# Attention and a 16-expert mixture in one kernel: combine weights computed from one set of instructions, two routing parts joined, key maxima kept from PSUM

## The chip, the cores and the metric

The kernel runs on one core of one Trainium2 chip. The metric is the device time of one launch in microseconds (us); lower is better. The core has five engines that run on their own and wait for one another through semaphores: PE (TensorE, matrix products; its weight loads are shown apart as PEld), DVE (VectorE), ACT (ScalarE), POOL (GpSimd) and SP (SyncE, which here issues nearly all transfers). Each engine takes its own instructions strictly in the order in which they were written for it, so an instruction that waits holds up everything behind it on that engine. Matrix products land in PSUM, a small memory of banks next to PE, and are read from there by ACT and DVE.

## The reference

Two stages. First an attention through 49 agents per batch (4 batches of 10048 tokens, 128 channels):

```
s  = scale * (agents @ k.T);  s -= max over keys;  a2k = exp(s) / (sum + 1e-9)
agent_v = a2k @ v
q2a = the same softmax of scale * (q @ agents.T), over the agents
x = q2a @ agent_v                       # 40192 x 128
```

Then a two-level mixture of experts on the 40192 rows of x: 4 groups with 4 experts each, hidden width 1024.

```
g_logits = x @ w_group;  g = argmax;  g_w = softmax(g_logits)[g]
e_logits = xg @ w_expert[g];  e = argmax;  e_w = softmax(e_logits)[e]
out[row] = g_w * e_w * (relu(x @ w1[g, e]) @ w2[g, e])
```

Both softmaxes carry the 1e-9 in the denominator. The product g_w * e_w is the *combine weight* of a row.

## The kernel before

**Tiling.** A batch has 79 blocks of 128 tokens; four blocks make a *tile* (512 tokens), so a batch has 20 tiles. A *unit* is one eighth of a tile's expert work: two 512-column products into a PSUM bank (`ph<-et,wbuf`), a ReLU on ACT (`hh<-ph`), its rounding rest on DVE (`hl<-ph,hh`), and, eight units later, twelve 128-column products (`po<-wbuf,hh` and `po<-wbuf,hl`). Inputs are handled as pairs of 16-bit numbers, a rounded part and a rest (`xh`, `xl`).

**Stages.** The first batch's keys and values are worked through alone (`front`). Then come the 20 tiles of the first, the second and the third batch (`SEQ = (1, 2, 3, 0)`), each with the one expert that most of that batch's tokens chose (`choose` finds it, loads its weights `w1f`, `w2f` and writes them into `wbuf` through `expert_split`). The fourth batch is sorted by expert, and its tiles run last, with the weights fetched per tile. All other work (keys and values of the later batches, queries, routing) is written between the units of the tiles by hand-made *lanes*: a list of generators with start and end times (`QUEUE`), advanced once per unit by `advance`, the lane furthest behind first. `k1` is the key lane of the second batch of `SEQ`, `q1` its query lane, `a1` its routing lane (`followed`). A scheduler of the framework then places each instruction on its engine, so the final order has to be read from the built program.

**Routing in parts.** `PARTS` and `SORTS` cut a batch's 20 tiles into parts: 0-2, 2-5, 5-10, 10-15, 15-20, or 0-5, 5-10, 10-15, 15-20 for the sorted batch. For each part `logits` computes the 20 router logits, `routing` the arg-max masks (`oh`), the first part's `choose` the batch's main expert, and `weigh` the combine weights `cw`. With n the token blocks of a part (8, 12 or 20), every DVE instruction of a part is 128 partitions by a small multiple of n. In `weigh` before, `numerators` runs once for the groups and once for the experts: subtract the largest, multiply by a per-token factor (both into a tile `rd`), exponentials on ACT (`rd<-rd,scb`); `fold` adds or takes the maximum of four rows in two steps (`rhg`, `rrg`, `rhe`, `rre`, `rhm`, `rrm`).

**Key scores.** Per chunk of ten blocks `key_scores` fills a PSUM bank (`at`) with 128x490 scores and ACT copies it to `S`. `key_largest`, one pipeline stage later, reduces the chunk over its ten blocks from `S` into `mch`; `key_max` reduces the eight chunk maxima (`mx<-mch`). PSUM tiles named `at` share three banks.

**Staging.** Key, query and expert loads share four staging buffers (tag `xf`: `xf<-kT`, `xf<-qT`, `w1f`); value loads and `w2f` share two (tag `vf`). SP issues all of them in one queue. `values_load(ei)` in `expert_load` makes SP read the chosen expert's number (`cei`) before it can issue `w1f`.

Of the kernel before, what the change touches and what calls it, by code (L numbers as in the profile page):

```python
# [10 lines left out]
F32 = mybir.dt.float32  # L11
F16 = mybir.dt.float16
I32 = mybir.dt.int32
AF = mybir.ActivationFunctionType
ALU = mybir.AluOpType
AX = mybir.AxisListType
# [4 lines left out]
P = 128  # L21
# [3 lines left out]
NA = 49  # L25
NG = 4
# [6 lines left out]
CT = 10  # L33
# [28 lines left out]
NOWN = B - 1  # L62
SORTED = SEQ[NOWN]
OT = -(-NT // TQ)
PARTS = ((0, 2), (2, 5), (5, 10), (10, 15), (15, OT))
SORTS = ((0, 5), (5, 10), (10, 15), (15, OT))
ST = 5 * TQ
ORDER = "kkkkkmkvkvqkqmvvqvvvv"
RATE = np.array([900.0, 1100.0])
# [66 lines left out]
def build(ctx, tc, qT, kT, v, agT, wr, w1, w2, cpk, out):  # L136
# [141 lines left out]
    def skewed(n, *stages):  # L278

        for i in range(n + len(stages) - 1):  # L280
            yield "chunk"
            live = [[stages[k](i - k), 0] for k in reversed(range(len(stages))) if 0 <= i - k < n]
            while live:
                moved = False
                for x in list(live):
                    if x[1] > clock[0] and not forced[0]:
                        continue
                    y = next(x[0], "end")
                    if y == 0:
                        continue  # L290
                    moved = True
                    if y == "end":
                        live.remove(x)
                        continue
                    if isinstance(y, int):
                        x[1] = clock[0] + y
                    yield
                if not moved:
                    yield 0
# [10 lines left out]
    def key_load(b, ci, early=None):  # L310

        st = state[b]
        if ci == 0:
            st["S"] = rt.tile([P, NT, NA], F32, name="S", tag="S")
            st["mch"] = sm.tile([P, len(chunks), NA], F32, name="mch")
            st["part"] = []
        st["k", ci] = yield from split_load("k", b, ci, early)
        yield

    def load_only(kind, b, ci):  # L320

        if (kind, b, ci) not in loaded:
            load_ahead((kind, b, ci))
        yield

    def key_scores(b, ci):

        st = state[b]
        S, mch = st["S"], st["mch"]
        t0, t1 = chunks[ci]  # L330
        xh, xl = st.pop(("k", ci))
        ps = bank()
        full = t1 - t0 - (1 if t1 == NT else 0)
        for t in range(t0, t1):
            scores(b, ps, xh, xl, t - t0, min(P, N - t * P))
            if t % 5 == 4:
                yield
        yield 1
        act.activation(S[:, t0:t0 + full], ps[:, 0:full * NA].rearrange("p (t a) -> p t a", a=NA), AF.Copy)
        if t1 == NT:  # L340
            act.activation(S[0:LAST, NT - 1], ps[0:LAST, full * NA:(full + 1) * NA], AF.Copy)
        yield

    def key_largest(b, ci):
# [9 lines left out]
    def key_max(b, c0, c1, early):  # L354

        st = state[b]
        i = len(st["part"])
        mx = sm.tile([P, NA], F32, name="mx")
        vec.tensor_reduce(out=mx, in_=st["mch"][:, c0:c1].rearrange("p c a -> p a c"), axis=AX.X, op=ALU.max)
        yield HOP  # L360
        ps = bank()
        pe.transpose(ps[0:NA, 0:P], mx, identf)
        yield HOP
        if i == 0:
            st["ma"] = sm.tile([NA, 3], F32, name="ma")
        ma = st["ma"][:, i:i + 1]
        vec.tensor_reduce(out=ma, in_=ps[0:NA, 0:P], axis=AX.X, op=ALU.max)
        dg = sm.tile([NA, NA], F32, name="dg")
        vec.tensor_scalar(out=dg, in0=identf[0:NA, 0:NA], scalar1=ma, scalar2=None, op0=ALU.mult)
        yield HOP  # L370
        ps = bank()
        pe.matmul(ps[:, 0:NA], ones[0:NA, :], dg, start=True, stop=True)
        yield HOP
        mb = sm.tile([P, 1, NA], F32, name="mb")
        vec.tensor_copy(out=mb[:, 0], in_=ps[:, 0:NA])
        if i == 0 and early:
            st["acc"] = bank(False)
        st["part"].append((c0, c1, mb, st["acc"][0:NA, i * (C + 1):(i + 1) * (C + 1)] if early else None))
        yield
# [107 lines left out]
    def agents(b):  # L487

        st = state[b]
        n = len(chunks)  # L490
        yield from skewed(n, lambda ci: load_only("k", b, ci), lambda ci: key_load(b, ci), lambda ci: key_scores(b, ci), lambda ci: key_largest(b, ci))
        yield from key_max(b, 0, n, False)
        yield from skewed(n, lambda ci: both(value_load(b, ci), value_less(b, ci)), lambda ci: value_exp(b, ci), lambda ci: value_split(b, ci), lambda ci: value_products(b, ci))
        yield
        acc = st["acc"]
        za = sm.tile([P, NA], F32, name="za2")
        vec.tensor_reduce(out=za, in_=acc[:, NA:(ZT + 1) * NA].rearrange("p (t a) -> p a t", a=NA), axis=AX.X, op=ALU.add)
        vec.tensor_scalar(out=za, in0=za, scalar1=1e-9 * ES, scalar2=None, op0=ALU.add)
        vec.reciprocal(out=za, in_=za)
        avT = sm.tile([P, NA], F32, name="avT")  # L500
        vec.scalar_tensor_tensor(out=avT, in0=acc[:, 0:NA], scalar=1.0 / VS, in1=za, op0=ALU.mult, op1=ALU.mult)
        yield
        yield from agents_scaled(b, avT)
# [116 lines left out]

    def followed(b):

        parts = SORTS if b == SORTED else PARTS
        first_part = 1 if b == SEQ[0] else 0
        moved = lambda f: lambda k: f(b, *parts[k + first_part])
        yield from skewed(len(parts) - first_part, *[moved(f) for f in ((part_logits, part_positions, part_rows) if b == SORTED else (part_logits, part_weights))])
        if b == SORTED:
            yield from order(b)
# [194 lines left out]
    def weigh(b, t0, t1):  # L823

        st = state[b]
        r = t0 // ST
        n, t = t1 - t0, slice(t0 - r * ST, t1 - r * ST)
        lg, ohf, g = st["lg", r], st["ohf", r], st["g", r]
        og = ohf[:, 0:NG, t]
        gm, zz, zr = [a[:, t] for a in g]  # L830

        def fold(src, op, name):
            h = sm.tile([P, 2, ST], F32, name="rh" + name)[:, :, 0:n]
            vec.tensor_tensor(out=h, in0=src[:, 0:2], in1=src[:, 2:4], op=op)
            r = sm.tile([P, ST], F32, name="rr" + name)[:, 0:n]
            vec.tensor_tensor(out=r, in0=h[:, 0], in1=h[:, 1], op=op)
            return r

        def numerators(x, largest):
            bc = lambda a: a.unsqueeze(1).broadcast_to([P, 4, n])  # L840
            d = sm.tile([P, 4, ST], F32, name="rd")[:, :, 0:n]
            vec.tensor_sub(out=d, in0=x, in1=bc(largest))
            vec.tensor_mul(out=d, in0=d, in1=bc(zr))
            yield HOP
            act.activation(d, d, AF.Exp, scale=st["scb"][:, 1:2])
            yield HOP
            return d

        x = sm.tile([P, NG, 4, ST], F32, name="rx")[:, :, :, 0:n]
        vec.tensor_mul(out=x, in0=lg[:, NG:NG + NE, t].rearrange("p (g e) t -> p g e t", g=NG), in1=og.unsqueeze(2).broadcast_to([P, NG, 4, n]))  # L850
        yield
        el = sm.tile([P, 4, ST], F32, name="rel")[:, :, 0:n]
        vec.tensor_add(out=x[:, 0:2], in0=x[:, 0:2], in1=x[:, 2:4])
        vec.tensor_add(out=el, in0=x[:, 0], in1=x[:, 1])
        yield
        sg = yield from numerators(lg[:, 0:NG, t], gm)
        sg = fold(sg, ALU.add, "g")
        yield
        se = yield from numerators(el, fold(el, ALU.max, "m"))
        se = fold(se, ALU.add, "e")  # L860
        yield
        vec.scalar_tensor_tensor(out=se, in0=se, scalar=1e-9, in1=zz, op0=ALU.add, op1=ALU.mult)
        vec.scalar_tensor_tensor(out=sg, in0=sg, scalar=1e-9, in1=se, op0=ALU.add, op1=ALU.mult)
        yield
        vec.reciprocal(out=sg, in_=sg)
        if t0 == 0:
            st["cw"] = sm.tile([P, NTP], F32, name="cw", bufs=3)
        cw, x0 = st["cw"][:, t0:t1], st["rows", r][:, t]
        vec.tensor_scalar(out=cw, in0=sg, scalar1=st["scb"][:, 1:2], scalar2=1.0 / W2S, op0=ALU.mult, op1=ALU.mult)
        vec.tensor_copy(out=x0[:, :, 2 * NA:2 * NA + 2].bitcast(F32), in_=cw.unsqueeze(2))  # L870
        sync.dma_start(out=erow[b].rearrange("(p t) c -> p t c", t=NTP)[:, t0:t1], in_=x0.bitcast(I32))
        yield
# [585 lines left out]
```

## Time and profile before

| | |
|---|---|
| time, median of 3 runs | 1004.84 us (1002.79 to 1009.59) |
| the profiled execution's own time | 1003.51 us |
| its span, first to last instruction | 1001.8 us |
| mean granted TensorE clock | 0.974 |
| PE, DVE, ACT, POOL busy | 90%, 78%, 64%, 43% of the span |

The 1.7 us between the profiled execution's time and its span lie outside the instructions. A granted clock below 1 means that the chip ran TensorE slower than it can for part of the time. "PE busy" is a modelled share: products are pipelined, so a busy PE need not be at its peak. The profile's line L131 is the helper through which all PE, DVE and ACT instructions pass, so rows are told apart by their tiles (`out<-in`), not by lines.

### The profile page before, as it was taken

How to read it: one execution, taken by the hardware profiler on the slowest of the kernel's cores; microseconds unless marked ns; L12 is line 12 of the kernel's file. 1: busy time of each engine (PE TensorE's matmuls, PEld its weight loads, DVE VectorE, ACT ScalarE, POOL GpSimd, SP SyncE). 2: the span in 40 equal slices, each digit the busy share in tenths (PEclk: the TensorE clock that was granted, in tenths of full speed). 3: DMA queues.
4: the chain of work that ended last, by engine and by line, in shares of the span. 5: the costliest groups of instructions: out<-in, count | busy, mean ns of one | idle time of the engine just before them, and what ended most of it. 6: DMA issues, size and time to landing. Idle time of an engine off the chain costs nothing.

```text
span 1001.8 us, 31196 instructions
## 1 busy us (share of the span) xinstructions
PE 900.1 (90%) x12947; PEld 718.8 (72%) x12948; DVE 784.7 (78%) x1758; ACT 636.3 (64%) x1086; POOL 426.2 (43%) x569
## 2 busy tenths in 40 slices
PE   3858898999878998989989989999999999999994
PEld 2735677787756776767777777787777877777884
DVE  5636899889949887799988889989987666666663
ACT  4507678776757765768776777666556565555552
POOL 3108644442641334553334443554555214444444
PEclk9977999999989999999999999999999999999998
DMA  9637514633454445362524420223535545554551
GB/s 308 188 105 209 170 62 122 188 92 100 122 172 124 140 123 148 89 185 64 149 89 128 142 70 26 104 72 100 174 120 200 184 148 183 188 178 149 174 194 33
DMA packets 107511, 138.14 MB, mean 138 GB/s; under 512 B 7479, under 2 KB 88186, under 8 KB 104160
## 3 DMA queue, kind: packets, MB, share of 16 engines
q1 hardware_dynamic: 102208, 125.75, 39.8%
q0 software_dynamic: 5152, 10.30, 3.1%
q8 instruction: 103, 1.69, 0.7%
q14 instruction: 48, 0.39, 0.1%
HBM read 96.83 MB, written 39.45 MB: 136 GB/s over the span
## 4 chain that ended last, share of the span: by engine, by line
PE 51%; DVE 27%; DMA 6%; POOL 5%; ACT 5%; issue 5%; SPq 1%; POOLq 0%; DVEq 0%; ACTq 0%
PE po L131 25%; PE ph L131 17%; DVE hl L131 10%; PE at L131 8%; POOL xl L267 4%; DVE vl L131 2%; DMA xf<-kT 2%; ACT hh L131 2%; DVE oh L131 1%; DVE oo L131 1%; DMA erow<-rows 1%; DVE rd L131 1%; DVE mq L131 1%; DVE ef L131 1%; DVE rx L131 1%
## 5 line engine op out<-in xcount | busy, mean ns | idle before, releaser
L131 DVE SCALAR_TENSOR_TENSOR hl<-ph,hh 128x512 f16<-128x512 f32 (+1 forms) x644 | 432.9, 680 | 122.7 <-ACT hh L131 121.2
L131 PEld LDWEIGHTS <-hh 128*128 128x128 f16 x5104 | 419.5, 98 | 146.9 <-issue 3.9
L131 PE MATMUL po<-wbuf,hh 128*128 128x128 f16 x5104 | 501.7, 220 | 0.0
L131 ACT ACTIVATE hh<-ph 128x512 f16<-128x512 f32 (+1 forms) x644 | 376.8, 592 | 194.5 <-PE ph L131 191.4
L131 PE MATMUL po<-wbuf,hl 128*128 128x128 f16 x2552 | 463.6, 220 | 0.0
L131 PE MATMUL ph<-et,wbuf 98*128 98x512 f16 (+2 forms) x1312 | 386.3, 377 | 26.9 <-DVE hl L131 25.1
L267 POOL TENSOR_TENSOR xl<-xf,xh 128x256 f16<-128x256 f32 x280 | 183.8, 691 | 211.1 <-ACT xh L131 168.1
L131 PEld LDWEIGHTS <-hl 128*128 128x128 f16 x2552 | 249.9, 98 | 0.8 <-issue 0.3
L131 PEld LDWEIGHTS <-wbuf 98*128 98x128 f16 (+1 forms) x1412 | 108.8, 100 | 53.0 <-issue 36.6
L1198 POOL DMA_INDIRECT out<-oo,er x82 | 80.2, 978 | 130.2 <-ACT hh L131 92.7
L975 POOL DMA_INDIRECT sorted_rows<-rows,slot x79 | 78.1, 989 | 63.1 <-ACT hh L131 44.4
L131 ACT ACTIVATE xh<-xf 128x1280 f16<-128x1280 f32 (+2 forms) x59 | 73.6, 1253 | 20.5 <-PE at L131 10.6
L693 POOL TENSOR_TENSOR rows<-ef,rows 128x245 f16<-128x245 f32 (+1 forms) x62 | 40.7, 678 | 70.5 <-ACT rows L131 69.2
L462 POOL TENSOR_TENSOR sl<-S,sh 128x245 f16<-128x245 f32 (+2 forms) x51 | 35.2, 714 | 79.7 <-ACT sh L131 70.0
L131 PE MATMUL at<-agh,xl 128*128 128x49 f16 x553 | 57.1, 187 | 8.9 <-POOL xl L267 8.8
L131 PEld LDWEIGHTS <-xh 128*128 128x128 f16 (+1 forms) x1164 | 55.8, 99 | 7.8 <-ACT xh L131 4.6
L131 PE MATMUL at<-agh,xh 128*128 128x49 f16 x553 | 57.1, 187 | 4.0 <-ACT xh L131 3.8
L131 PEld LDWEIGHTS <-xl 128*128 128x128 f16 (+1 forms) x582 | 48.9, 98 | 12.3 <-POOL xl L267 12.0
L131 PE MATMUL at<-agl,xh 128*128 128x49 f16 x553 | 56.7, 187 | 0.0
L131 ACT ACTIVATE et<-at 98x512 f16<-98x512 f16 (+2 forms) x81 | 47.0, 584 | 13.8 <-PE at L131 9.7
L131 DVE SCALAR_TENSOR_TENSOR vl<-vf,vh 128x640 f16<-128x640 f32 (+2 forms) x51 | 43.0, 849 | 5.5 <-ACT vh L131 5.5
L131 DVE TENSOR_TENSOR oo<-po,cw 128x512 f32<-128x512 f32 (+1 forms) x60 | 40.3, 672 | 3.4 <-PE po L131 3.4
(254 smaller groups left out, 940.9 us busy)
## 6 DMA issues: line engine op xcount, KB each, us to landing
wbuf<-wdr SPq DMA_DIRECT2D x22, 1024.0 KB, 4.7
vf<-v SPq DMA_DIRECT2D x28, 640.0 KB, 4.5
xf<-qT SPq DMA_DIRECT2D x28, 640.0 KB, 4.1
xf<-kT SPq DMA_DIRECT2D x23, 640.0 KB, 4.3
out<-oo SPq DMA_DIRECT2D x57, 256.0 KB, 3.3
erow<-rows SPq DMA_DIRECT2D x13, 510.0 KB
er<-sorted_rows SPq DMA_DIRECT2D x19, 256.0 KB, 3.1
wbuf<-kT SPq DMA_DIRECT2D x5, 640.0 KB, 5.3
```

The source lines that it names most:

```text
L131: return f(*a, **k)
L267: pool.tensor_sub(out=xl[:, a:z], in0=xf[:, a:z], in1=xh[:, a:z])
L462: pool.tensor_sub(out=sl[0:m, y][:, z], in0=x[:, z], in1=sh[0:m, y][:, z])
L693: pool.tensor_sub(out=x0[:, a:z, NA:2 * NA], in0=ef[:, a:z], in1=x0[:, a:z, 0:NA])
L975: ins = pool.indirect_dma_start(out=sorted_rows[:, :], out_offset=bass.IndirectOffsetOnAxis(ap=at, axis=0), in_=x, in_offset=None, bounds_ ...
L1198: ins = pool.indirect_dma_start(out=out, out_offset=bass.IndirectOffsetOnAxis(ap=to, axis=0), in_=y, in_offset=None, bounds_check=B * N - ...
```

## The change

Three edits:

1. `weigh` stacks the group logits and the expert logits of a part in one tile `rd` of eight rows. The factor is multiplied in once over eight rows, ACT takes one exponential over eight rows, and the two sums are folded together. The maximum of the expert logits is still taken by itself.
2. The parts 0-2 and 2-5 are kept apart only for the first batch. The second and the third batch now use 0-5, as the sorted batch did.
3. For the three later batches a running maximum `most` of 128x490 is kept: DVE copies the first chunk's scores out of PSUM and takes the elementwise maximum of it and of each later chunk's bank. `key_largest` is left out of their pipeline, which is a stage shorter, and `key_max` reduces `most` (128x490) once. The first batch keeps `mch`.

```diff
-PARTS = ((0, 2), (2, 5), (5, 10), (10, 15), (15, OT))
 SORTS = ((0, 5), (5, 10), (10, 15), (15, OT))
+PARTS = ((0, 2), (2, 5), *SORTS[1:])
...
     def key_scores(b, ci):
...
+        if "most" in st:
+            yield
+            for i, z, m in ((0, full, P), (full, t1 - t0, LAST)):
+                if z > i:
+                    o, x = st["most"][0:m, i:z], ps[0:m, i * NA:z * NA].rearrange("p (t a) -> p t a", a=NA)
+                    if ci == 0:
+                        vec.tensor_copy(out=o, in_=x)
+                    else:
+                        vec.tensor_tensor(out=o, in0=x, in1=o, op=ALU.max)
         yield
...
     def key_max(b, c0, c1, early):
...
-        vec.tensor_reduce(out=mx, in_=st["mch"][:, c0:c1].rearrange("p c a -> p a c"), axis=AX.X, op=ALU.max)
+        vec.tensor_reduce(out=mx, in_=(st["mch"][:, c0:c1] if early else st["most"]).rearrange("p c a -> p a c"), axis=AX.X, op=ALU.max)
...
     def agents(b):
-        yield from skewed(n, lambda ci: load_only("k", b, ci), lambda ci: key_load(b, ci), lambda ci: key_scores(b, ci), lambda ci: key_largest(b, ci))
+        yield from skewed(n, lambda ci: load_only("k", b, ci), lambda ci: key_load(b, ci), lambda ci: key_scores(b, ci))
...
     def followed(b):
-        parts = SORTS if b == SORTED else PARTS
+        parts = PARTS if b == SEQ[0] else SORTS
...
     def weigh(b, t0, t1):
...
+        four = lambda a: a.unsqueeze(1).broadcast_to([P, 4, n])
         x = sm.tile([P, NG, 4, ST], F32, name="rx")[:, :, :, 0:n]
         vec.tensor_mul(out=x, in0=lg[:, NG:NG + NE, t].rearrange("p (g e) t -> p g e t", g=NG), in1=og.unsqueeze(2).broadcast_to([P, NG, 4, n]))
         yield
-        el = sm.tile([P, 4, ST], F32, name="rel")[:, :, 0:n]
+        d = sm.tile([P, 2, 4, ST], F32, name="rd")[:, :, :, 0:n]
         vec.tensor_add(out=x[:, 0:2], in0=x[:, 0:2], in1=x[:, 2:4])
-        vec.tensor_add(out=el, in0=x[:, 0], in1=x[:, 1])
-        yield
-        sg = yield from numerators(lg[:, 0:NG, t], gm)
-        sg = fold(sg, ALU.add, "g")
-        yield
-        se = yield from numerators(el, fold(el, ALU.max, "m"))
-        se = fold(se, ALU.add, "e")
-        yield
+        vec.tensor_sub(out=d[:, 0], in0=lg[:, 0:NG, t], in1=four(gm))
+        yield
+        vec.tensor_add(out=d[:, 1], in0=x[:, 0], in1=x[:, 1])
+        h = sm.tile([P, 2, 2, ST], F32, name="rh")[:, :, :, 0:n]
+        vec.tensor_max(out=h[:, 0], in0=d[:, 1, 0:2], in1=d[:, 1, 2:4])
+        yield
+        vec.tensor_max(out=h[:, 1, 0], in0=h[:, 0, 0], in1=h[:, 0, 1])
+        vec.tensor_sub(out=d[:, 1], in0=d[:, 1], in1=four(h[:, 1, 0]))
+        yield
+        flat = d.rearrange("p k e t -> p (k e) t")
+        vec.tensor_mul(out=flat, in0=flat, in1=zr.unsqueeze(1).broadcast_to([P, 8, n]))
+        yield HOP
+        act.activation(flat, flat, AF.Exp, scale=st["scb"][:, 1:2])
+        yield HOP
+        vec.tensor_add(out=h, in0=d[:, :, 0:2], in1=d[:, :, 2:4])
+        sums = sm.tile([P, 2, ST], F32, name="rs")[:, :, 0:n]
+        vec.tensor_add(out=sums, in0=h[:, :, 0], in1=h[:, :, 1])
+        yield
+        sg, se = sums[:, 0], sums[:, 1]
         vec.scalar_tensor_tensor(out=se, in0=se, scalar=1e-9, in1=zz, op0=ALU.add, op1=ALU.mult)
```

**What it moves: SP's queue.** The rows below are SP's, in the key phase of the third batch (lane `k2`), where the second batch's expert is loaded before the change. `cei` is the chosen expert's number, `xf<-kT` a chunk of keys, `erow` the routing rows sent out, `oo` a finished tile.

```order
L237 DMA xf<-kT 128x1280 x2
L871 DMA erow_124<-rows 128x408
L1187 DMA out<-oo 128x4x128
L1079 TENSOR_LOAD cei
L1082 ISA
L1082 DMA w1f<-w 128x1024
L1083 ISA
L1083 DMA w2f<-w 128x8x128
L237 DMA xf<-kT 128x1280 x2
L416 DMA vf<-v 128x10x128
L237 DMA xf<-kT 128x1088
```

After the change the same load stands here, three finished tiles later (17 tiles are stored ahead of it instead of 14).

```order
L1194 DMA out<-oo 128x4x128
L428 DMA vf<-v 128x10x128
L1086 TENSOR_LOAD cei
L1089 ISA
L1089 DMA w1f<-w 128x1024
L1090 ISA
L1090 DMA w2f<-w 128x8x128
L237 DMA xf<-qT 128x1280
L237 DMA xf<-qT 128x1088
L1194 DMA out<-oo 128x4x128
L237 DMA xf<-kT 128x1280
L428 DMA vf<-v 128x10x128
```

Before, three key chunks stood behind the expert's load; after, the keys of that batch are all loaded ahead of it, and two query chunks and then values stand behind it.

**What it moves: the expert's weights on DVE.** The rows are DVE's around the writing of the second batch's weights (`wbuf_120`; `w1` halves first, then the halves of `w2`). Before:

```order
L131 TENSOR_TENSOR wbuf_120<-at,wbuf_120 128x512
L131 SCALAR_TENSOR_TENSOR wbuf_120<-w2f,wbuf_120 128x4x128
L131 TENSOR_TENSOR oo<-po,cw 128x512
L131 SCALAR_TENSOR_TENSOR hl<-ph,hh 128x512 x2
L131 SCALAR_TENSOR_TENSOR wbuf_120<-w2f,wbuf_120 128x4x128
L131 SCALAR_TENSOR_TENSOR hl<-ph,hh 128x512
```

After (128x384 is the size of the batch's last, shorter tile):

```order
L131 TENSOR_TENSOR wbuf_120<-at,wbuf_120 128x512
L131 TENSOR_REDUCE mq<-at 128x10
L131 SCALAR_TENSOR_TENSOR hl<-ph,hh 128x384
L131 TENSOR_TENSOR ef<-at,mq 128x490
L131 COPY rows<-cw 128x20
L131 SCALAR_TENSOR_TENSOR vl<-vf,vh 128x640
L131 SCALAR_TENSOR_TENSOR hl<-ph,hh 128x384 x2
L131 SCALAR_TENSOR_TENSOR wbuf_120<-w2f,wbuf_120 128x4x128
L131 SCALAR_TENSOR_TENSOR hl<-ph,hh 128x384
L131 TENSOR_TENSOR oo<-po,cw 128x512
L131 SCALAR_TENSOR_TENSOR wbuf_120<-w2f,wbuf_120 128x4x128
```

Counted in units on PE, the second `w1` half's product (`at<-w1f`) stood 26 units ahead of the second batch's first `ph<-et,wbuf_120` and now stands 4 ahead; for the third batch it stood 30 ahead and now 4. From `cei` on DVE to the first of these products it is 7 units now (11 before) for the second batch, and 8 (10 before) for the third.

**What it takes away: a part on DVE.** The rows are DVE's in the first batch's part 5-10, from the multiplication by the factor to the first of the two closing instructions, other lanes' work between them. Before:

```order
L131 TENSOR_TENSOR rd<-rel,rrm 128x80
L131 SCALAR_TENSOR_TENSOR vl<-vf,vh 128x640
L131 TENSOR_TENSOR rd<-rd,zr 128x80
L131 SCALAR_TENSOR_TENSOR hl<-ph,hh 128x512
L131 TENSOR_TENSOR ef<-at,mq 128x490
L131 TENSOR_TENSOR rhe<-rd 128x40
L131 SCALAR_TENSOR_TENSOR hl<-ph,hh 128x512
L131 TENSOR_TENSOR rre<-rhe 128x20
L131 SCALAR_TENSOR_TENSOR vl<-vf,vh 128x640
L131 SCALAR_TENSOR_TENSOR rre<-rre,zz 128x20
```

After:

```order
L131 TENSOR_TENSOR rd<-rd,rh 128x80
L131 TENSOR_TENSOR ef<-at,mq 128x490
L131 TENSOR_TENSOR rd<-rd,zr 128x160
L131 SCALAR_TENSOR_TENSOR hl<-ph,hh 128x512
L131 SCALAR_TENSOR_TENSOR vl<-vf,vh 128x640
L131 TENSOR_TENSOR rh<-rd 128x80
L131 SCALAR_TENSOR_TENSOR hl<-ph,hh 128x512
L131 TENSOR_TENSOR rs<-rh 128x40
L131 SCALAR_TENSOR_TENSOR rs<-rs,zz 128x20
```

The instructions for the group softmax that stood further up (`rd<-rd,zr`, `rhg<-rd`, `rrg<-rhg`, each of its own) are gone; the remaining ones are twice as wide. Over the whole program DVE has 1424 rows instead of 1546 (of which a repeated row counts once), ACT 796 instead of 813, and PE the same 26498.

More of the change, by code (lines that the diff above doesn't have):

```diff
@@ L314, in key_load @@
             st["S"] = rt.tile([P, NT, NA], F32, name="S", tag="S")
-            st["mch"] = sm.tile([P, len(chunks), NA], F32, name="mch")
+            if early:
+                st["mch"] = sm.tile([P, len(chunks), NA], F32, name="mch")
+            else:
+                st["most"] = rt.tile([P, CT, NA], F32, name="most")
             st["part"] = []
@@ L328, in key_scores @@
         st = state[b]
-        S, mch = st["S"], st["mch"]
+        S = st["S"]
         t0, t1 = chunks[ci]
@@ L341, in key_scores @@
             act.activation(S[0:LAST, NT - 1], ps[0:LAST, full * NA:(full + 1) * NA], AF.Copy)
+        if "most" in st:
[5 more added lines that the diff above has]
+                        vec.tensor_copy(out=o, in_=x)
+                    else:
+                        vec.tensor_tensor(out=o, in0=x, in1=o, op=ALU.max)
         yield
@@ L830, in weigh @@
         gm, zz, zr = [a[:, t] for a in g]
[L832 to L847, printed above, removed]
+        four = lambda a: a.unsqueeze(1).broadcast_to([P, 4, n])
         x = sm.tile([P, NG, 4, ST], F32, name="rx")[:, :, :, 0:n]
```

## Prediction

> **What bounds the kernel now.** I read the page first, its busy table and its chain.
>
> ```profile
> PE 900.1 (90%) x12947; PEld 718.8 (72%) x12948; DVE 784.7 (78%) x1758; ACT 636.3 (64%) x1086; POOL 426.2 (43%) x569
> PE 51%; DVE 27%; DMA 6%; POOL 5%; ACT 5%; issue 5%; SPq 1%; POOLq 0%; DVEq 0%; ACTq 0%
> ```
>
> PE leads, but the chain that ended last lies 27% on DVE, 270 us of the 1001.8. To see where, I cut the span at the turns of the batches with the view of windows (columns: stretch, length, busy us of PE, PEld, DVE, ACT, POOL, granted clock, transfer share, GB/s).
>
> ```profile
> 78.00:287.00 209.00, 186.84 (x2943) 149.28 (x2944) 177.94 (x388) 151.41 (x253) 109.20 (x166) 0.95 0.45 136
> 287.00:517.00 230.00, 208.41 (x3240) 167.33 (x3237) 196.81 (x411) 162.68 (x275) 90.15 (x135) 0.98 0.42 124
> 517.00:700.00 183.00, 172.27 (x2601) 137.97 (x2601) 165.82 (x436) 129.05 (x235) 85.52 (x118) 0.99 0.29 92
> 700.00:1002.00 302.00, 288.59 (x3690) 228.28 (x3687) 205.53 (x390) 164.22 (x283) 127.19 (x130) 0.99 0.47 160
> ```
>
> From 700 us on PE is busy 288.6 of 302: nothing that DVE saves there counts. Everything that the change touches lies in the three rows above, 622 us with PE at 567.5, so **54.5 us of PE idle time** is all there is to win. DVE is busy 540.6 there, 87%, nearly as much as PE. If its 270 us of chain lie in these 622, about 0.43 of each DVE microsecond is on the chain. Of the waits in 78 to 700 (waiter, releaser, total us, times, longest) three bear on the change.
>
> ```profile
> PE ph L131 <- DVE hl L131: 25.1, 28, 2.1
> ACT rd L131 <- DVE rd L131: 31.6, 26, 2.7
> PE at L131 <- DVE ef L131: 2.0, 2, 1.1
> ```
>
> PE's largest wait, 25.1 us, is for DVE to free a bank of hidden rows. ACT stands 31.6 us at the head of its queue with an exponential of `weigh` until DVE has made its input.
>
> **The change, part by part: key maxima.** The view of groups, shapes apart, gives busy us and mean ns of one.
>
> ```profile
> L131 DVE TENSOR_REDUCE mch<-S 128x49 f32<-128x490 f32 x28 | 27.8, 992 | 4.2 <-ACT S L131 4.2
> L131 DVE TENSOR_REDUCE mch<-S 128x49 f32<-128x392 f32 x4 | 3.3, 830 | 0.2 <-ACT S L131 0.2
> L131 DVE TENSOR_TENSOR ef<-at,mq 128x490 f32<-128x490 f32 x28 | 18.6, 663 | 0.4
> L131 DVE TENSOR_REDUCE mx<-mch 128x49 f32<-128x392 f32 x3 | 2.4, 810 | 0.0
> ```
>
> The maximum of a PSUM bank with `most` is not in the trace; the nearest row is `ef<-at,mq`, PSUM with an SBUF operand, same size: 663 ns. The three later batches have 21 full chunks and 3 short ones: 21 x (992 - 663) = 6.9 us and, scaled to 392 columns, 3 x 0.3 = 0.9. The final reduction grows from 392 to 490 elements, 3 x (992 - 810) = 0.5 back. Net 7 us; ends 0 (a price like `mch`'s own) and 10.
>
> What it may cost is the bank: ACT's copy alone freed it, now DVE's maximum must have run too, behind whatever stands ahead in DVE's queue. Query banks are freed by DVE in this way already, in the `ef` row of the waits: 2.0 us of PE in all. I charge the key banks the same 2 us. The page "PSUM — Partial Sum Buffer" of the Trainium skill, section "PSUM bank collisions raise a hardware error", has it that no two engines may access one bank's quadrant at once, so copy and maximum must follow one another. By that rule, with PE waiting each time, the cost would be an estimated 24 x 0.66 = 16 us; no run here shows such a collision.
>
> **Sharing the softmaxes.** The rows at n = 20:
>
> ```profile
> L131 DVE TENSOR_TENSOR rd<-rd,zr 128x80 f32<-128x80 f32 x26 | 7.1, 274 | 0.1
> L131 DVE TENSOR_TENSOR rhg<-rd 128x40 f32<-128x40 f32 x13 | 2.9, 221 | 0.0
> L131 DVE TENSOR_TENSOR rrg<-rhg 128x20 f32<-128x20 f32 x13 | 3.5, 272 | 0.0
> L131 DVE TENSOR_TENSOR rhe<-rd 128x40 f32<-128x40 f32 x13 | 3.1, 237 | 0.0
> L131 DVE TENSOR_TENSOR rre<-rhe 128x20 f32<-128x20 f32 x13 | 2.3, 175 | 0.2
> L131 DVE TENSOR_TENSOR rx<-rx 128x160 f32<-128x160 f32 x13 | 4.6, 356 | 0.1
> L131 DVE TENSOR_TENSOR rel<-rx 128x80 f32<-128x80 f32 x13 | 3.5, 273 | 0.0
> ```
>
> Gone: 2 x 274 + 221 + 272 + 237 + 175 = 1453 ns. In their place one of 160 columns (356, as `rx<-rx`), one of 80 (273, as `rel`), one of 40 (237, as `rhe`): 866 ns. That is 0.59 us a part. Thirteen parts with n = 20 stay: 7.6 us; the first batch's two small parts add 1.2 by the same figure.
>
> ACT runs 17 exponentials in place of 38, because 19 parts become 17 with one each. ACT's own time is hidden (443 of 622 us busy in the windows). About half of its 31.6 us of waiting goes, but ACT is 5% of the chain, so I count nothing; if that cover fails, the gain is larger, not smaller.
>
> **Joining the parts.** For two batches the sets at n = 8 and n = 12 become one at n = 20. Three instructions at the three sizes:
>
> ```profile
> L131 DVE TENSOR_TENSOR rx<-lg,oh 128x320 f32<-128x320 f32 x13 | 6.2, 481 | 0.0
> L131 DVE TENSOR_TENSOR rx<-lg,oh 128x192 f32<-128x192 f32 x3 | 1.0, 347 | 0.0
> L131 DVE TENSOR_TENSOR rx<-lg,oh 128x128 f32<-128x128 f32 x3 | 0.8, 283 | 0.0
> L131 DVE TENSOR_TENSOR oh<-oh 128x320 f16<-128x320 f16 x13 | 4.8, 370 | 0.0
> L131 DVE TENSOR_TENSOR oh<-oh 128x192 f16<-128x192 f16 x3 | 0.9, 288 | 0.0
> L131 DVE TENSOR_TENSOR oh<-oh 128x128 f16<-128x128 f16 x3 | 1.1, 371 | 0.0
> L131 DVE TENSOR_TENSOR rre<-rhe 128x12 f32<-128x12 f32 x3 | 0.5, 166 | 0.1
> L131 DVE TENSOR_TENSOR rre<-rhe 128x8 f32<-128x8 f32 x3 | 1.3, 420 | 0.1
> ```
>
> 347 + 283 - 481 = 149, 288 + 371 - 370 = 289, 166 + 420 - 175 = 411: mean 283 ns. `routing` and `weigh` have some 28 such instructions, so a join saves 7.9 us, with the sharing 8.5, twice 17.
>
> DVE loses 7 + 7.6 + 1.2 + 17 = **33 us**. On the chain that is 33 x 0.43 = 14. It is bounded by 0 (PE late everywhere) and the 25.1 us wait. PE is late next in many places, with 91% busy, so I take 10.
>
> **What moves.** The second batch's expert load leaves the middle of the key phase. The view of the chain in order of time there (start, us, what), then ACT's timeline row, then a window:
>
> ```profile
> 270.60 0.15 DVE cei L131
> 271.32 0.35 SPq L1082
> 272.46 6.67 DMA xf<-kT
> 293.27 5.96 POOL xl L267 x10
> 279.24 1.27 ACT L131 ACTIVATE xh<-xf 128x1280 f16<-128x1280 f32 x1 [3.63 <-DMA xf<-kT]
> 268.00:287.00 19.00, 13.44 (x206) 10.48 (x203) 10.98 (x20) 10.40 (x16) 11.94 (x19) 0.82 0.67 210
> ```
>
> SP can issue `w1f` at 271.32 only after `cei` at 270.60, and the keys behind it leave at 272.46 and land 6.7 us later; ACT waits for them, PE behind ACT, and the clock falls to 0.82. PE loses 19 - 13.4 = 5.6 us and 0.18 x 13.4 = 2.4 in speed, 8 in all. After the change no key waits behind `cei`. Keys still share four buffers and POOL's splitting (`xl`, 293.27), so I take 4 of 0 to 8.
>
> In exchange both experts get ready just before their batch begins.
>
> ```profile
> DMA to landing us min/median/max: 5.0/5.2/7.6
> 243.55 0.38 SPq L1187 DMA_DIRECT2D out<-oo  x1
> 253.67 0.38 SPq L1187 DMA_DIRECT2D out<-oo  x1
> ```
>
> Two tiles are stored 10.1 us apart, 1.27 us a unit. From `cei` to the first product of `w1f` there are now 7 units, 8.9 us, and 8 units, 10.2. The load needs 0.7 us to its issue and 5.2 (up to 7.6, of `w2f`, its twin) to land: 5.9 to 8.3. It fits, with 0.6 to 3 us to spare. Behind `w1f` on SP are queries and values: `w2f` holds one of two value buffers until the turn of the batch, so values are loaded one at a time there. I charge 1 us (0, if all is in time; the rival's price below, if not).
>
> **Sum.** 10 + 4 - 2 - 1 = 11 us off the profiled execution's own 1003.5 us: **992.5 us**. The profiled execution lies 1.3 us under the median of the runs shown, 1004.84, which itself spreads over 6.8 us; I leave that in the range.
>
> **The rivals.**
>
> *PE hides it, or small instructions are cheap.* `rre<-rhe` at 128x12 takes 166 ns and at 128x20 175: taken alone, eight columns are 9 ns, and the 420 at 128x8 then is waiting for an input that other work fills. If so, joining and sharing give almost nothing, and 7 us of key maxima remain, 3 on the chain, with the other terms +1: 999.5 us. For it speaks PE at 91%, against it the 25.1 us of PE waiting for DVE. The page "Vector Engine (DVE) Microarchitecture Reference" of the Trainium skill, section "Measured stream behaviour on trn2 (trn3 not measured)", goes this way: some 75 ns per instruction beside 1.04 ns a column. By it sharing would save an estimated 0.23 us a part and a join 2.1, 7 us with the rest; the rows above are two to three times longer.
>
> *The weights come late.* Slower than before: `w1f` lands after PE has reached its product, at both turns. It decides when `cei` to landing passes 8.9 and 10.2 us, an SP queue blocked for 1 to 3 us by a store or a value load ahead. The price can be seen at the program's start, where nothing covers the same load:
>
> ```profile
> PE at L131 <- DMA w1f<-w: 6.0, 1, 6.0
> 50.00:75.00 25.00, 12.83 (x89) 9.49 (x87) 8.20 (x50) 1.92 (x5) 0.00 (x0) 0.74 0.33 105
> ```
>
> PE waits 6.0 us, and the granted clock of that stretch is 0.74, up to 0.26 x 25 = 6.5 us more: 12.5 a turn, 25 for two. 1003.5 - 10 + 25 = 1018.5 us. Against it: the margins above.
>
> *The key banks bind.* The change would not relieve DVE's users, since PE waits for `most` behind a full DVE queue, 0.66 us for each of 24 chunks, 16 us in place of 2: 1006.5 us. Against it: the `ef` wait.
>
> *All of it counts.* PE gets the full 25.1 us back, less 2 for the banks and 1 for the turns, and the whole 8 us of the key phase: 30 us, 973.5; more likely four fifths, 979.5 us. For it speaks ACT's halved waiting, which feeds PE too.
>
> **How the numbers follow.** A measurement of this kernel tells about 1% from no change: under 994.8 us is faster, over 1014.9 slower. The forecast gets 0.52 (its own range 984 to 1000; seven tenths of it under 994.8: 0.36 faster, 0.16 the same), hidden or cheap 0.20 (same), late weights 0.09 (0.08 slower, 0.01 same), banks 0.05 (same), all of it 0.14 (faster). That is 0.50 faster, 0.42 the same, 0.08 slower. For 8 in 10 the range runs from 977 us, inside the last case, to 1009, past the banks' case; the late weights and the best of the last case stay outside.
>
> **What would show it.** DVE's busy time in the profile falls by about 33 us, with PE's unchanged; `most<-at,most` near 663 ns; `rd<-rd,zr` at 128x160 near 356; ACT's wait for `rd` about halved; PE's wait for `hl` under 18 us; no half-speed clock near 280 us, and none at the two turns. I am wrong if DVE's busy time falls and PE's wait for `hl` does not, if `at<-w1f` shows a wait for its transfer near the turns, or if PE's waits for `most` add up to more than a few us.

## The result and the profile after

The changed kernel takes **989.58 us** (median of 4 runs, 987.92 to 993.08), the kernel before 1005.32 beside it: ratio 0.985 [0.9827, 0.9874], 1.5% faster. The profiled execution took 989.52 us, its span is 987.7. On some of the chips used below the kernel before itself takes 1015 to 1018 us, so every kernel is compared with it on its own chip, by the ratio.

The page's busy table after the change:

```profile
PE 894.9 (91%) x12947; PEld 715.3 (72%) x12948; DVE 761.6 (77%) x1647; ACT 628.9 (64%) x1063; POOL 430.1 (44%) x569
```

DVE lost 23.1 us (784.7 before), not 33. The waits of 78 to 700 us (waiter, releaser, total us, times, longest):

```profile
PE ph L131 <- DVE hl L131: 22.9, 26, 3.0
ACT rd L131 <- DVE rd L131: 21.6, 14, 3.9
PE at L131 <- DVE ef L131: 6.5, 5, 3.1
PE at L131 <- DVE most L131: 0.3, 1, 0.3
```

PE waits for `hl` nearly as long as before (25.1). So most of the gain of 14 us in these two profiles must lie elsewhere. It shows when one looks at *where* the kernel gets ahead. I took the start of each tile as the start of the first of its eight `hh<-ph` on ACT, and subtracted that of before (us; tiles 0 to 19 are those of the first batch in `SEQ`, 20 to 39 of the second, 40 to 59 of the third):

| tile (start before) | 2 (103.5) | 14 (252.8) | 18 (314.6) | 40 (593.2) | last `hh` (985.5) |
|---|---|---|---|---|---|
| after | -0.4 | +3.5 | -9.9 | -14.4 | -14.9 |
| after, a second profile | -3.1 | +0.7 | -12.7 | -16.5 | -17.1 |

Tiles 14 to 18 alone bring 13.3 us in both, and they stand around the place where the expert's load left the key phase. From tile 2 to 14 the changed kernel *lost* 3.8 us. The view of windows there, before and then after (columns as in the prediction):

```profile
253.00:268.00 15.00, 13.71 (x240) 11.04 (x238) 14.76 (x39) 11.57 (x19) 11.33 (x19) 1.00 0.38 115
287.00:303.00 16.00, 15.20 (x229) 11.40 (x227) 9.47 (x15) 12.05 (x20) 5.96 (x10) 1.00 0.49 152
```

```profile
253.00:268.00 15.00, 14.75 (x261) 12.14 (x259) 10.18 (x19) 11.58 (x19) 6.71 (x11) 1.00 0.22 67
268.00:287.00 19.00, 18.64 (x343) 15.18 (x340) 11.61 (x19) 16.29 (x28) 17.76 (x30) 1.00 0.54 163
287.00:303.00 16.00, 15.87 (x235) 12.70 (x233) 15.73 (x37) 10.77 (x19) 4.14 (x7) 1.00 0.08 24
```

In the middle stretch PE is busy 18.64 us of 19 instead of 13.44, and the granted clock of 0.82 is back at 1.00. The stretches on both sides gain too, 1.0 and 0.7 us, which the prediction had not counted.

### The profile page after: what moved, and what is told of

It is laid out like the page before. It is cut to its first block, busy times and chain, and to the rows that moved or that the text cites. A ratio compares the mean times of both kernels' runs of the same rounds, so it can differ in the third digit from the quotient of the medians.

```text
span 987.7 us, 31082 instructions
## 1 busy us (share of the span) xinstructions
PE 894.9 (91%) x12947; PEld 715.3 (72%) x12948; DVE 761.6 (77%) x1647; ACT 628.9 (64%) x1063; POOL 430.1 (44%) x569
## 5 line engine op out<-in xcount | busy, mean ns | idle before, releaser
L131 PE MATMUL ph<-et,wbuf 98*128 98x512 f16 (+2 forms) x1312 | 384.6, 376 | 24.5 <-DVE hl L131 22.9
L131 ACT ACTIVATE et<-at 98x512 f16<-98x512 f16 (+2 forms) x81 | 47.3, 585 | 16.2 <-PE at L131 12.9
L131 DVE SCALAR_TENSOR_TENSOR vl<-vf,vh 128x640 f16<-128x640 f32 (+2 forms) x51 | 45.0, 891 | 5.8 <-ACT vh L131 5.8
```

The source lines that it names most:

```text
L131: return f(*a, **k)
```

## The experiments

Two theories stood against each other. The **work theory** is the prediction's main term: each microsecond taken from DVE brings about 0.3. The **place theory**: the gain is the expert's load leaving the keys' way, and DVE's work is worth little.

### One edit at a time

`e1_shared` is the kernel before with the new `weigh`, `e2_joined` with the joined parts, `e3_maxima` with the key maxima; `e4_not_joined` is the changed kernel with the parts kept apart. The core of each:

```diff
 e1_shared, against before: weigh as in the change
-        sg = yield from numerators(lg[:, 0:NG, t], gm)
...
-        se = yield from numerators(el, fold(el, ALU.max, "m"))
+        vec.tensor_mul(out=flat, in0=flat, in1=zr.unsqueeze(1).broadcast_to([P, 8, n]))
...
 e3_maxima, against before: key_scores, key_max and agents as in the change
+                        vec.tensor_tensor(out=o, in0=x, in1=o, op=ALU.max)
...
 e2_joined, against before
-        parts = SORTS if b == SORTED else PARTS
+        parts = PARTS if b == SEQ[0] else SORTS
 e4_not_joined, against after
-        parts = PARTS if b == SEQ[0] else SORTS
+        parts = SORTS if b == SORTED else PARTS
```

The expectations, in this order:

> The kernel before with the shared softmaxes alone (parts and key maxima as before). Work theory (each DVE microsecond taken away brings about 0.3 us, wherever it stood): some 9 us of DVE time go, so 2.7 us less than the kernel before, about 1002.5 us. Place theory (what counts is that the expert's load leaves the key phase, which comes from the joined parts alone): within 2 us of the kernel before. PE's wait for hl: 22 us by the first, 25 by the second.

> The kernel before with the parts 0-2 and 2-5 joined for the second and third batch, nothing else. Work theory: 17 us of DVE time go, 5 us of them on the chain, and 3 net for the moved load: 8 us less, about 997 us. Place theory: nearly the whole gain of the full change, 12 to 16 us less, 989 to 993 us, and no half-speed clock near 280 us.

> The kernel before with the running key maxima alone. Work theory: 7 us of DVE time go, 2 us on the chain, and 2 back for the banks: 1005 us, no change. Place theory: no change either. A loss of over 3 us would show that the banks held for DVE cost more than the 2 us charged; PE's wait for most is then over 3 us.

> The changed kernel with the parts 0-2 and 2-5 kept apart for every batch, that is shared softmaxes and running maxima together. Work theory: 16 us of DVE time go, 5 on the chain, 2 back: about 1002 us. Place theory: the expert's load stands in the key phase again, the stall near 280 us is back, and the time is within 3 us of the kernel before, about 1005 us.

| | median us | ratio to before (1004.55) | DVE busy us | ahead in tiles 2-14 / 14-18 / 18-40 / 40-end |
|---|---|---|---|---|
| e1 shared | 1005.12 | 1.0004 [0.9989, 1.0018] | 773.0 | +2.2 / +1.3 / -0.9 / +0.7 |
| e2 joined | 997.98 | 0.9941 [0.9924, 0.9958] | 771.0 | +0.3 / -9.6 / -1.9 / +6.5 |
| e3 maxima | 1000.80 | 0.9968 [0.995, 0.9985] | 779.5 | +0.6 / -1.3 / -3.7 / +0.7 |
| e4 shared, maxima | 1000.93 | 0.9965 [0.9948, 0.9982] | 769.5 | +3.9 / -3.2 / -1.7 / -2.6 |

(Minus is gained.) `e1` took 11.7 us of work from DVE and gained nothing in the end, where the work theory had 2.7 us. `e3` took the least, 5.2 us, and gained 3.8, which neither theory had. `e2` and `e4` came out near the totals of the work theory (997 and 1002 us), but `e2` by gains and losses in places that this theory does not know. There is no fixed price per microsecond of DVE. In the waits of `e1` from 78 to 700 us ACT's wait for `rd` is halved, and PE's for `hl` has not fallen:

```profile
PE ph L131 <- DVE hl L131: 27.7, 30, 6.4
ACT rd L131 <- DVE rd L131: 16.2, 12, 2.4
```

But the zero of `e1` is a sum. From tile 18 to 24 it gets 10.7 us ahead; at the start of tile 39 it is still 7.6 us ahead of the kernel before, and it loses 8.0 us in that one tile. There (574 to 596 us) DVE's queue is held up by two small fills of query buffers that wait until POOL is done with the buffers, and PE waits 6.4 us for the `hl` behind them. In the kernel before DVE stands idle before neither of these two fills.

```profile
PE ph L131 <- DVE hl L131: 7.2, 3, 6.4
DVE xf L131 <- POOL xl L267: 5.1, 2, 3.0
```

All other waits for `hl` in `e1` add up to 21.3 us, about the 22 that the work theory expected. `advance` paces the lanes by DVE's and ACT's counted work, so an edit of DVE's instructions also moves all others, and `e1` can't tell less work from another order. In `e4`, with 15.2 us less of DVE's work than before, no single wait stands out, and the total is still not smaller:

```profile
PE ph L131 <- DVE hl L131: 28.2, 31, 3.0
```

Only the join, which moves the load, has the large gain in tiles 14 to 18, and `e1` and `e3` still have the stall there, with the granted clock at 0.82 as before; `e4` has it a little later, at 0.79 from 287 to 303 us. The view of windows, `e1` and then `e2`:

```profile
268.00:287.00 19.00, 13.42 (x209) 10.62 (x208) 11.07 (x21) 11.10 (x16) 11.97 (x20) 0.82 0.67 210
```

```profile
268.00:287.00 19.00, 19.00 (x360) 15.72 (x358) 15.41 (x23) 15.76 (x27) 17.07 (x28) 1.00 0.46 139
```

But `e2` gives 4.9 us back between tile 58 and the end; that is taken up below.

### The load's place, and the buffer it takes

`e5_late_choose` is the kernel before, parts apart, with the second and third batch's `choose` after part 2-5 instead of part 0-2, so that the load stands where it does after the change (two small DVE instructions more). `e6_own_buffers` is the kernel before with `w1f` and `w2f` of these two batches loaded into a weight buffer that is free at that time. `e7_after_own` does this to the changed kernel.

```diff
 e5
-        if i0 == 0:
+        if i0 == (0 if b == SEQ[0] else PARTS[1][0]):
             yield from choose(b)
...
 e6, e7
+        if b in SEQ[1:NOWN]:
+            raw = wbuf[(SEQ.index(b) + 1) % NB].bitcast(F32)
+            w1f, w2f = raw[:, 0:F], raw[:, F:2 * F].rearrange("p (k c) -> p k c", c=C)
...
```

> The kernel before with its parts as they were, but the second and third batch choose their expert in the part 2-5, from the counts of both parts. DVE's work is that of before and two small instructions more; the expert's load stands where the full change puts it (first product at tile 19.1 and 39.1 of the PE order). Place theory: most of the gain without any work taken away, 8 to 14 us less, 991 to 997 us. Work theory: 4 us for the key phase less 1 for the turns, 3 us less, about 1002 us.

> The kernel before, the load of the second and third batch's expert where it was, but into the weight buffer of another batch that is free then, instead of one of the four staging buffers of the keys and one of the two of the values. If the key phase is held up because w1f sits in a staging buffer, the stall from 272 to 300 us goes and the time falls by 6 to 10 us. If it is held up because the keys stand behind cei in SP's queue and land late, the first wait of 3.6 us stays, and the time falls by less than 4 us.

> The changed kernel with the expert loads in the free weight buffers, as in the run on the kernel before. If the value buffer that w2f holds until the turn of the batch costs about 1 us a turn, 1 to 3 us less than the changed kernel, 987 to 989 us; if nothing waits for it, the same 989.6 us.

Measured (before: 1017.74): `e5` 1015.55, ratio 0.9974 [0.9956, 0.9991]; `e6` 1007.00, 0.9887 [0.9873, 0.9901]; `e7` 1002.26, 0.9851 [0.9837, 0.9865]. Own buffers bring 11 us to the kernel before. `e7` stands at the ratio that the changed kernel had on another chip (0.985); the changed kernel itself was not run on this one. If the ratio carries over, own buffers bring nothing to it, and the join and the own buffers remove one and the same stall. `e5` gained 10.3 us from tile 14 to 18, as the place theory says, and then lost most of it; its whole gain of 2.6 us by the ratio refutes that theory as the whole account. The work theory's total of 3 us came out, but not by its account of 4 us for the key phase. 6.7 us are lost between tiles 18 and 40, where `e6` on the same chip loses 0.3; 3.9 of them at the next turn, where `e5`'s tile 19 takes 16.1 us against 12.2 before. The rest I have not traced.

Then the two loads apart, all of the change but the join on top of own buffers, and the changed kernel once more:

```diff
 e8 (w1f only)                                    e9 is the same for w2f
-        w1f = stg.tile([P, F], F32, name="w1f", tag="xf")
+        raw = wbuf[(SEQ.index(b) + 1) % NB].bitcast(F32) if b in SEQ[1:NOWN] else None
+        w1f = stg.tile([P, F], F32, name="w1f", tag="xf") if raw is None else raw[:, 0:F]
```

> The kernel before, but w1f of the second and third batch goes into a part of a free weight buffer; w2f still takes one of the two value buffers. Both own buffers together gained 11 us. Key-buffer theory (w1f holds one of the four buffers in which keys are staged, so two chunks of keys come late): all of it, 10 to 11 us. Value-buffer theory (w2f halves the value buffers, and the values' transfer stands ahead of later keys in SP's queue): nothing, 0 to 2 us. If the two add up, each gives about half.

> The twin: only w2f of the second and third batch goes into a free weight buffer, w1f still takes a key buffer. Key-buffer theory: 0 to 2 us. Value-buffer theory: 10 to 11 us.

> All of the change but the joined parts (shared softmaxes and key maxima, 3.5 us faster than before by themselves), with both expert loads in free weight buffers (11 us by itself). If the join gains only by moving the load out of the key phase, this is as fast as the changed kernel: 15 us under before. If the join's 17 us of DVE work count as well, as the work theory has it at 0.3 us each, this stays 5 us behind the changed kernel.

> The changed kernel once more, word for word, beside the others on one chip. All theories: ratio 0.985 to the kernel before.

| | median us | ratio to before (1005.35) | tiles 2-14 / 14-18 / 18-40 / 40-end |
|---|---|---|---|
| e8 w1f own | 994.40 | 0.9896 [0.9879, 0.9912] | +1.9 / -8.9 / -0.6 / -0.1 |
| e9 w2f own | 1005.63 | 0.9994 [0.9972, 1.0015] | +2.0 / +0.4 / 0.0 / +0.2 |
| e10 shared, maxima, own | 993.97 | 0.9893 [0.987, 0.9916] | +5.4 / -10.0 / -2.8 / -2.5 |
| e11 after again | 988.99 | 0.9856 [0.9836, 0.9876] | +3.8 / -13.3 / -3.8 / -0.6 |

The key-buffer theory's numbers came out to the microsecond: taking `w1f` out of the *key* buffers brings all of the 11 us, taking `w2f` out of the value buffers nothing. From tile 18 on `e8` runs like the kernel before. SP's part of the timeline shows what changed (start us, us, what, count), first the kernel before:

```profile
263.02 0.34 SPq L237 DMA_DIRECT2D xf<-kT  x1
...
271.32 0.35 SPq L1082 DMA_DIRECT2D w1f<-w  x1
271.87 0.41 SPq L1083 DMA_DIRECT2D w2f<-w  x1
272.46 1.52 SPq L237 DMA_DIRECT2D xf<-kT  x2
...
283.80 0.33 SPq L237 DMA_DIRECT2D xf<-kT  x1
```

and `e8`, where `wbuf<-w` is the load of `w1f`:

```profile
262.08 6.62 SPq L237 DMA_DIRECT2D xf<-kT  x3
269.00 0.34 SPq L871 DMA_DIRECT2D erow<-rows  x1
272.70 0.33 SPq L237 DMA_DIRECT2D xf<-kT  x1
...
274.05 0.34 SPq L1083 DMA_DIRECT2D wbuf<-w  x1
...
275.85 0.34 SPq L237 DMA_DIRECT2D xf<-kT  x1
```

With one buffer more for keys, the scheduler places two further key chunks *ahead* of the expert's load in SP's queue. Before, three chunks stood behind it, and the last of them left at 283.80; here one does, and it leaves at 275.85. Freeing the buffer thus also changed the place, and these runs cannot price the two apart. `e9` shows that the load's being ahead of the keys costs as before when only the key buffer is still taken:

```profile
268.00:287.00 19.00, 13.03 (x202) 10.24 (x200) 11.48 (x22) 9.92 (x15) 11.79 (x20) 0.87 0.50 157
```

`e10` says what the join has beyond this. With the stall gone in another way, sharing and maxima add 0.4 us (994.40 to 993.97), though they take 15 us of DVE's work, and the changed kernel is still 5.0 us ahead. That is the figure the work theory gave for the join; after `e1` I do not read it as its proof, since over 3 us of the difference between the two profiles stand in tiles 14 to 18 again. What of it is work and what is order stays open.

### A second wait at the end: the sorted batch

If sharing is worth nothing, putting the old `weigh` back should make the changed kernel no slower. `e12_two_edits` is that: joined parts and key maxima alone.

```diff
 e12, against after: the whole weigh
-        d = sm.tile([P, 2, 4, ST], F32, name="rd")[:, :, :, 0:n]
+        sg = yield from numerators(lg[:, 0:NG, t], gm)
+        sg = fold(sg, ALU.add, "g")
...
```

> The changed kernel with the separate softmaxes of before put back: the joined parts and the key maxima remain. By themselves these two gained 6.6 and 3.7 us, and the shared softmaxes nothing; alone and with the key maxima, the shared softmaxes came with a second batch that reached its tile 14 later by 2 to 4 us. Work theory (0.3 us for each us of DVE work): 3 us slower than the changed kernel, ratio 0.988 to before. Additive theory (each edit is worth what it gained alone): 10 us under before, 0.990. Place theory, with the shared softmaxes costing their 2 to 4 us in the tiles up to 14 and gaining nothing: 2 to 4 us faster than the changed kernel, 0.981 to 0.983, and so faster than both, if the last batch's weights do not come late, which cost the joined parts by themselves 5 us.

Measured: 1007.43 against 1015.30, ratio 0.9919 [0.99, 0.9939]. It is slower than the changed kernel. The work theory (0.988) and the place theory (0.981 to 0.983) missed, and the additive theory's 0.990 lies on the edge of the interval. The place theory had excepted the case that the last batch's weights come late, and they do. The waits near the end say why, `e2` from 765 to 800 us, then `e12` from 775 to 815:

```profile
PE ph L131 <- DMA wbuf<-wdr: 3.3, 1, 3.3
```

```profile
PE ph L131 <- DMA wbuf<-wdr: 4.9, 1, 4.9
```

PE stands waiting for the first weights that the fourth, sorted batch fetches. Neither the kernel before nor the changed one has this wait. What holds the fetch is a run of 79 scatters of routed rows on POOL. The rows of that tile's view (duration min/median/max, first and last start), before, after, `e2` and `e12`:

```profile
L975 POOL DMA_INDIRECT sorted_rows<-rows,slot x79: 969/978/1291, 636.6 to 785.0; - x79
```

```profile
L982 POOL DMA_INDIRECT sorted_rows<-rows,slot x79: 965/981/1536, 614.3 to 765.6; - x79
```

```profile
L975 POOL DMA_INDIRECT sorted_rows<-rows,slot x79: 966/982/1437, 628.0 to 779.7; - x79
```

```profile
L987 POOL DMA_INDIRECT sorted_rows<-rows,slot x79: 966/982/1132, 628.9 to 784.4; - x79
```

SP fetches the rows and then the weights after the last scatter: at 785.81 us in `e2`,

```profile
785.81 2.40 SPq L1122 DMA_DIRECT2D wbuf<-wdr  x2
```

and at 772.57 in the changed kernel. In `e2` PE comes to these tiles 10.6 us earlier than before, the last scatter only 5.3 us earlier, and so the wait opens. After the change the scatters begin 22 us earlier and end 19 us earlier, more than PE's 15. So the three edits do not simply add up: the join takes out the first stall, and sharing and the key maxima together get the scatters out of the way of the time so won. Counted from the start of tile 40, the first scatter comes after 35 us in every profile of a kernel that has both (after, `e4`, `e7`, `e10`, `e11`), after 43 to 44 us in before, `e3`, `e5`, `e6`, `e8` and `e9`, and after 46 to 47 us in `e1`, `e2` and `e12`. Sharing alone (`e1`) thus makes them later, not earlier; why the pair makes them earlier was not found, and sharing with the join alone was not tried. `e12` loses 8.0 us from tile 58 to the end, about its whole distance to the changed kernel (0.0069 of 1005, 6.9 us); `e7`, also profiled on a slower chip, loses 0.2 there.

## Why the prediction was right or wrong

The time came 3 us under the forecast of 992.5, inside the forecast's own range, but **the two main terms of the sum were mis-sized in opposite ways**, so that it came so near is partly luck. On the chip of `e8` to `e11` the gain of 16.4 us splits into 11.0 for the stall (`e8`), 0.4 for sharing and maxima beyond it (`e10`) and 5.0 that come with the join and are not traced to work or order.

- *DVE's work, 10 us.* Wrong, in two steps. The busy time fell by 23.1, not 33: sharing and maxima were sized fairly (11.7 and 5.2 us alone for 8.8 and 7), but the join, 13.7 alone, took only 7.9 more once the softmaxes were shared (769.5 to 761.6). Rows of the view of groups that the change leaves alone also grew, such as this one from 481 ns:

```profile
L131 DVE TENSOR_TENSOR rx<-lg,oh 128x320 f32<-128x320 f32 x15 | 8.2, 550 | 0.0
L131 DVE TENSOR_TENSOR rd<-rd,zr 128x160 f32<-128x160 f32 x15 | 5.2, 345 | 0.2
L131 DVE TENSOR_TENSOR most<-at,most 128x490 f32<-128x490 f32 x18 | 11.9, 659 | 3.0 <-ACT S L131 3.0
L131 DVE TENSOR_REDUCE mx<-most 128x49 f32<-128x490 f32 x3 | 3.0, 1004 | 0.1
```

  The worse step is the factor 0.43, DVE's share of the chain spread evenly over its work. (It divides the 270 us by the 622 us of time; by DVE's 540.6 busy us it would be 0.50.) The runs show no such price: 15 us of DVE's work are worth 0.4 us between `e8` and `e10`, 11.7 us nothing in the end in `e1`, and 5.2 us 3.8 us in `e3`; what a stretch gains can be lost at a wait elsewhere, as in tile 39 of `e1`. My own sign of error, "DVE's busy time falls and PE's wait for `hl` does not", is what happened: 25.1 to 22.9, where I said under 18, and 28.2 in `e4`. The rival "PE hides it" came nearest here: it had almost nothing for sharing and 3 us for the maxima, but it gave the join almost nothing too. The price in the Trainium skill's "Vector Engine (DVE) Microarchitecture Reference", "Measured stream behaviour on trn2", by which I estimated that DVE would save 7 us in all, is too low against the 23 us of busy time measured here.
- *The transfer stall, 4 of 0 to 8 us.* Right about the place and about the transfers that come late, only in part about why, and wrong in size. I put the wait down to the keys' standing behind `cei` in SP's queue; in `e8` `w1f` leaves no earlier than before (274.05 us, 271.32 before), and another buffer for it, with the order in SP's queue that follows from this, is enough to remove the stall. `e8` measures 11 us for the stall, beyond my upper bound, since I priced the one window from 268 to 287 us. In tiles 14 to 18 of one profile it is 8.9 us for `e8`, 10.0 for `e10` and 13.3 for the changed kernel. The sign that I gave came true: the clock from 268 to 287 us is 1.00 after the change.
- *The key banks, -2 us.* PE waits 0.3 us for `most`, and `e3` gained 3.8 us. The durations were right (659 and 1004 ns; 663 and 992 forecast). The 16 us that I estimated from "PSUM — Partial Sum Buffer" of the Trainium skill, "PSUM bank collisions raise a hardware error", did not come: in the trace of the changed kernel each maximum starts after ACT's copy of the same bank has ended, so the two do follow one another, but PE waits 0.3 us for it, not 16. PE's wait for the query banks (`ef`) did grow, from 2.0 to 6.5 us.
- *The hand-over, -1 us.* At the second batch's turn `at<-w1f` waits 2.5 us, for DVE and not for its transfer, as this row of PE's timeline shows:

```profile
322.83 2.08 PE L131 MATMUL at<-w1f,at 128*128 128x512 f32 x2 [2.53 <-DVE wbuf L131]
```

  So "the weights come late" did not happen, and the 1 us was about right: tiles 19 and 39 take 1.0 us longer each than before, 1.1 and 0.2 in the second profile. I was wrong that no slow clock would show at this turn. The windows of this turn, after and then before:

```profile
318.00:331.20 13.20, 10.67 (x136) 8.08 (x135) 11.74 (x30) 9.68 (x19) 3.18 (x5) 0.87 0.76 244
```

```profile
327.00:340.00 13.00, 10.88 (x156) 9.44 (x153) 10.99 (x24) 9.34 (x19) 5.47 (x8) 0.87 0.49 147
```

  The clock is 0.87 in both, so it is not of the change's making.

- *ACT's wait for `rd`* fell by a third (31.6 to 21.6), not by half, and `e1`, where it fell to 16.2, was no faster in the end.
- *Not in the prediction:* the scatters of the sorted batch, and a loss in tiles 2 to 14 of every kernel that has both the shared softmaxes and the key maxima (3.8 us in both profiles after, 3.9 in `e4`, 4.3 in `e7`, 5.4 in `e10`). About 2 us of it lie in the one profile of before with which all are compared: `e5`, `e6`, `e8` and `e9`, which do the same work as before up to there, lose 1.6 to 2.6 us too. Where the rest comes from was not found.

## What to carry to other kernels

A share of the chain is no price: find the stretches in which the bound engine truly stands idle, see what it waits for there, and count only the instructions that end that wait. When an edit nets nothing, look whether it gained in one place and lost in another, as `e1` did. When a load with a late address shares a rotating buffer with a stream, look at what is queued behind it; a buffer of its own was worth 1.0 to 1.1% here, more than any one of the three edits alone. And compare kernels tile by tile, not by their ends alone: a stage that gets ahead runs into the next late producer, and an edit that is worth nothing alone can, together with another, be what keeps that producer ahead.

## What was not expected of the hardware

Chips differ by about 1% for one program. The kernel before has medians of 1004.55 and 1005.35 us where `e1` to `e4` and `e8` to `e11` ran, and 1017.74 and 1015.30 where `e5` to `e7` and `e12` did. The changed kernel with own buffers (`e7`) was 12.2 us ahead of the profile of before at tile 40 and 4.9 at tile 54, so on that chip the third of the batches lost 7 us that `e11` lost only 1.5 of. The same stretch takes the other three kernels profiled on the slower chips, `e5`, `e6` and `e12`, 4.8 to 8.1 us longer than the profile of before, and no kernel on the others more than 1.7; why was not found. The ratios fit one that does not depend on the chip: 0.9887 for `e6` there and 0.9896 for `e8` elsewhere, 0.9851 for `e7` there and 0.985 and 0.9856 for the changed kernel elsewhere. No kernel but the one before was run on both, so this is not shown.
